# Chunk-selected attention in front of an expert layer: the attention part rewritten from single heads with 128-wide tiles to pairs of heads with 512-wide tiles

## The chip, the cores and the metric

The kernel runs on one core of a Trainium2 chip. The metric is device time in microseconds (us) of one execution. The core has five engines with queues of their own: PE multiplies matrices (its weight loads are listed apart as PEld), DVE and ACT work element by element and can read PE's output memory (PSUM), POOL works element by element on SBUF alone, and SP issues the DMAs. Each works through its queue in order; semaphores make one wait for another.

## The reference, cut to what matters

The first half is attention over 4 batches of 8 heads, 768 positions, head size 64. The keys of a head are cut into 24 chunks of 32. For each query an upper bound of its score with each chunk is made from the chunk's largest and smallest key, and only the six best chunks that are causally allowed are kept.

```python
    k_min = np.min(k_chunks, axis=3)
    k_max = np.max(k_chunks, axis=3)
    ub = np.sum(np.maximum(q[:, :, :, None, :] * k_min[:, :, None, :, :], q[:, :, :, None, :] * k_max[:, :, None, :, :]), axis=-1)
    ub = np.where(causal, ub, -1000000000.0)
    top_chunks = np.argsort(ub, axis=-1)[..., -top_k:]
    mask = sel & (pos[:, None] >= pos[None, :])
    scores = np.where(mask, scores, -1000000000.0)
    ...
    attn = attn / (np.sum(attn, axis=-1, keepdims=True) + 1e-09)
```

The second half takes the 3072 x 512 attention output as `x`: a dense two-layer network, plus one of 8 expert networks per row, chosen by the largest gate logit and weighted by its softmax probability. The kernel computes all 8 experts for all rows and multiplies by a gate vector that is zero except for the chosen one.

## The kernel before, in words

A tile framework orders the instructions of each engine by its own scheduling and puts in the semaphores; the program is fully unrolled. There are three stages, one after the other.

**Attention** (lines 80 to 166) goes head by head, 32 of them. Three DMAs bring q, k and v of a head (L84 to L86), 192 KB each. ACT casts q to float16 (L90), DVE casts k and v (L91, L92); v gets a 65th column of ones (L93), so that the product with it also gives the softmax's sum. PE turns k's six 128-row tiles (L99) and DVE copies each into `lhsT` (L100), whose rows 64 to 87 hold `expand`, which chunk a key belongs to (L96). DVE takes each chunk's maximum and minimum (L103, L108). Then, for each of six query tiles: PE turns q (L117), DVE copies it (L119), ACT makes its positive and negative parts (L121, L122), PE makes the bounds `ub` from them (L126, L127), and DVE selects in eight small instructions of 24 columns (L129 to L138). ACT scales the selection to 0 or -30000 (L140), PE turns it (L143), DVE copies it below the q rows in `rhs` (L144), so that one product gives scores and mask. For each key tile up to the diagonal PE makes 128x128 scores `sp` (L149), ACT takes the exponential `ex` (L154), DVE multiplies the diagonal tile by a triangle (L156), and PE multiplies with v (L157). DVE divides by the sum (L161, L162) into `xbig`.

**Weights** (L168 to L191): 72 pieces of 256 KB and a small one come by DMA into three staging buffers (L183) and are cast to float16 by DVE (L184). The order of every queue has them behind the attention; only the first three DMAs do not wait for a cast.

**Experts** (L193 to the end of the function): for six groups of 512 rows PE turns x (L211), ACT copies it out (L212), and for the dense network and each of 8 experts PE runs 16 products of 512 columns into `hp` (L242), ACT applies relu (L246), PE runs 16 into `yp` (L250), ACT scales by the gate (L258), DVE accumulates (L259). 24 DMAs write the output.

PE's order within a query tile is a chain that leaves PE three times before the first score (to DVE and ACT for `rhs` and `qrel`, to DVE and ACT for `selb`, to DVE for the mask rows of `rhs`); the scheduler interleaves the chains of several tiles, as far as the two or three buffers of each kind allow. A DVE or ACT instruction stands in its queue behind those of the other chains.

Of the kernel before, what the change touches and what calls it, by code (L numbers as in the profile page):

```python
# [8 lines left out]
FP = mybir.dt.float32  # L9
BF = mybir.dt.bfloat16  # L10
HF = mybir.dt.float16
# [6 lines left out]
def kernel(  # L18
# [22 lines left out]
    const = ctx.enter_context(tc.tile_pool(name="const", bufs=1))  # L41

    ident = const.tile([128, 128], HF)
    make_identity(nc, ident)
    identb = const.tile([128, 128], BF)
    make_identity(nc, ident)

    upptri = const.tile([128, 128], HF)
    make_upper_triangular(nc, upptri, 1.0, diag=True)

    expand = const.tile([NC, S], HF)
    nc.gpsimd.memset(expand, 1.0)
    nc.gpsimd.affine_select(out=expand, in_=expand, compare_op=ALU.is_ge, fill=0.0,
                            base=0, pattern=[[1, S]], channel_multiplier=-32)
    nc.gpsimd.affine_select(out=expand, in_=expand, compare_op=ALU.is_ge, fill=0.0,
                            base=31, pattern=[[-1, S]], channel_multiplier=32)

    causal01 = const.tile([128, NT, NC], FP)
    causalbias = const.tile([128, NT, NC], FP)
    nc.gpsimd.memset(causal01, 1.0)  # L60
    nc.gpsimd.affine_select(out=causal01, in_=causal01, compare_op=ALU.is_ge, fill=0.0,
                            base=0, pattern=[[128, NT], [-32, NC]], channel_multiplier=1)
    nc.gpsimd.memset(causalbias, 0.0)
    nc.gpsimd.affine_select(out=causalbias, in_=causalbias, compare_op=ALU.is_ge, fill=NEG,
                            base=0, pattern=[[128, NT], [-32, NC]], channel_multiplier=1)

    xbig = const.tile([128, NM, Dm], HF)

    with (
        tc.tile_pool(name="aload", bufs=3) as aload,  # L70
        tc.tile_pool(name="ahead", bufs=2) as ahead,
        tc.tile_pool(name="aq", bufs=3) as aq,
        tc.tile_pool(name="aexp", bufs=3) as aexp,
        tc.tile_pool(name="pt", bufs=2, space=bass.MemoryType.PSUM) as pt,
        tc.tile_pool(name="psc", bufs=2, space=bass.MemoryType.PSUM) as psc,
        tc.tile_pool(name="pout", bufs=2, space=bass.MemoryType.PSUM) as pout,
        tc.tile_pool(name="psmall", bufs=1, space=bass.MemoryType.PSUM) as psmall,
    ):
        for b in range(B):
            for h in range(H):  # L80
                qf = aload.tile([128, NT, D], FP)
                kf = aload.tile([128, NT, D], FP)
                vf = aload.tile([128, NT, D], FP)
                nc.sync.dma_start(out=qf, in_=q[b, h].rearrange("(t p) d -> p t d", p=128))  # L84
# [30 lines left out]
                for t in range(NT):  # L115
# [31 lines left out]
                    for bb in range(t + 1):  # L147
# [7 lines left out]
                        if bb == t:  # L155
                            nc.vector.tensor_mul(ex, ex, upptri)  # L156
# [140 lines left out]
```

## Time and profile before

| what | value |
|---|---|
| time, median of 2 runs (lowest, highest) | 1068.89 us (1068.28, 1069.51) |
| profiled execution, first to last instruction | 1067.7 us |
| PE busy, matmuls | 790.1 us, 74% |
| DVE busy | 611.5 us, 57% |
| ACT busy | 576.1 us, 54% |
| POOL busy | 4.8 us |
| attention, until the last `xbig` (L162) | 0 to 568 us |
| weights, until PE's first transpose of `xbig` (L211) | 568 to 652 us |
| experts | 652 to 1067.7 us |

The page gives the profiled execution no time beside this span; the median lies 1.2 us above it. Busy time is the union of an engine's instruction spans. The span of an instruction is its own duration, from reading to the write's end; two that follow each other without a wait can overlap, so the spacing of their starts is smaller than the duration. A PE matmul's listed end is modelled. "Clock" is the share of full TensorE speed that was granted, as the profile has it.

### The profile page before, as it was taken

What the parts mean: (1) busy time and instruction counts of PE and PEld (TensorE: products, weight loads), DVE (VectorE), ACT (ScalarE), POOL (GpSimd) and SP (SyncE); (2) the same over time, 40 slices, a digit from 0 to 9 for tenths busy, and PEclk for the clock granted to TensorE, in tenths of its full rate; (3) what the DMA queues carried; (4) which work ended last, traced back from release to release, by engine and by line L of the source; (5) the groups of instructions that cost most, each with busy time, mean ns of one, the idle gap of its engine ahead of it and who ended that gap; (6) DMA issues with size and microseconds to landing.
All of it is one profiled execution on the core that took longest, in us unless ns stands there. A gap on an engine that the chain in (4) does not pass through costs nothing.

```text
span 1067.7 us, 14836 instructions
## 1 busy us (share of the span) xinstructions
PE 790.1 (74%) x4224; PEld 382.4 (36%) x4224; DVE 611.5 (57%) x3297; ACT 576.1 (54%) x1857; POOL 4.8 (0%) x17
## 2 busy tenths in 40 slices
PE   4667767676776767676762005999999999999998
PEld 2333333333333333333330002444444444444443
DVE  6777777877777777777874332433333434433234
ACT  3545544454444445454441003777777777777676
POOL 1000000000000000000000000000000000000000
PEclk9999999999999999999999999999999999999899
DMA  7111111112111111100005772000010010100101
GB/s 178 38 31 45 23 46 28 40 23 45 30 38 31 37 31 38 35 19 1 1 1 150 219 223 86 1 12 28 1 41 1 1 40 1 40 1 1 40 1 40
DMA packets 89699, 45.01 MB, mean 42 GB/s; under 512 B 77329, under 2 KB 77329, under 8 KB 89617
## 3 DMA queue, kind: packets, MB, share of 16 engines
q1 hardware_dynamic: 89616, 44.07, 15.1%
q8 instruction: 33, 0.54, 0.2%
q14 instruction: 50, 0.40, 0.1%
HBM read 37.77 MB, written 6.29 MB: 41 GB/s over the span
## 4 chain that ended last, share of the span: by engine, by line
PE 59%; DVE 19%; ACT 10%; DMA 7%; issue 4%; SPq 0%; ACTq 0%; DVEq 0%
PE hp L242 18%; PE yp L250 17%; PE op L157 7%; DMA s<-in_moe_w_dram 7%; ACT ex L154 6%; PE sp L149 5%; DVE rhs L144 3%; PE qtp L117 3%; PE pst L143 3%; PE tp L99 2%; DVE work L134 2%; ACT selb L140 2%; DVE sel L136 1%; DVE xbig L162 1%; DVE sel L138 1%
## 5 line engine op out<-in xcount | busy, mean ns | idle before, releaser
L259 DVE TENSOR_TENSOR acc<-acc,ts 128x512 f32<-128x512 f32 x192 | 130.8, 693 | 233.5 <-ACT ts L258 233.5
L154 ACT ACTIVATE ex<-sp 128x128 f16<-128x128 f32 x672 | 163.2, 275 | 134.2 <-PE sp L149 118.4
L157 PE MATMUL op<-v_sb,ex 128*128 128x65 f16 x672 | 147.1, 237 | 44.4 <-ACT ex L154 25.4
L149 PE MATMUL sp<-rhs,lhsT 88*128 88x128 f16 x672 | 151.6, 293 | 35.2 <-DVE rhs L144 32.0
L250 PE MATMUL yp<-w2e,hT 128*128 128x512 f16 x768 | 173.6, 379 | 0.0
L242 PE MATMUL hp<-xT,w1e 128*128 128x512 f16 x768 | 173.6, 379 | 0.0
L246 ACT ACTIVATE hT<-hp 128x512 f16<-128x512 f32 x216 | 129.0, 597 | 56.7 <-PE hp L242 56.4
L258 ACT ACTIVATE ts<-yp,gvec 128x512 f32<-128x512 f32 x192 | 130.0, 687 | 40.1 <-PE yp L250 40.1
L250 PEld LDWEIGHTS <-hT 128*128 128x128 f16 x864 | 80.1, 98 | 106.3 <-ACT hT L246 17.1
L157 PEld LDWEIGHTS <-ex 128*128 128x128 f16 x672 | 69.5, 106 | 132.6 <-ACT ex L154 66.3
L140 ACT ACTIVATE selb<-sel 128x24 f16<-128x24 f32 x192 | 42.3, 221 | 125.8 <-DVE sel L138 124.5
L242 PEld LDWEIGHTS <-w1e 128*128 128x128 f16 x768 | 75.2, 98 | 90.6
L143 PE MATMUL pst<-ident,selb 128*24 128x128 f16 x192 | 54.0, 281 | 56.7 <-ACT selb L140 54.3
L211 PE MATMUL tp<-ident,xbig 128*128 128x128 f16 x96 | 19.7, 239 | 94.3 <-ACT xT L212 94.2
L149 PEld LDWEIGHTS <-lhsT 88*128 88x128 f16 x672 | 72.0, 115 | 35.8 <-issue 23.7
L212 ACT ACTIVATE xT<-tp 128x128 f16<-128x128 f16 x96 | 22.3, 275 | 94.1 <-DVE w2e L184 84.9
L99 PE MATMUL tp<-ident,k_sb 128*64 128x128 f16 x192 | 56.9, 306 | 8.2 <-DVE k_sb L91 4.8
L121 ACT ACTIVATE qrel<-qtp 64x128 f16<-64x128 f16 x192 | 50.7, 264 | 20.3 <-DVE rhs L119 20.2
L117 PE MATMUL qtp<-ident,q_sb 128*64 128x128 f16 x192 | 54.9, 301 | 7.4 <-ACT qrel L122 3.6
L144 DVE COPY rhs<-pst 24x128 f16<-24x128 f16 x192 | 41.4, 216 | 25.4 <-PE pst L143 18.7
L156 DVE TENSOR_TENSOR ex<-ex,upptri 128x128 f16<-128x128 f16 x192 | 42.3, 220 | 22.8 <-ACT ex L154 19.6
L162 DVE TENSOR_SCALAR xbig<-op,rs 128x64 f16<-128x64 f32 x192 | 53.6, 279 | 1.0
(62 smaller groups left out, 856.8 us busy)
## 6 DMA issues: line engine op xcount, KB each, us to landing
s<-in_moe_w_dram SPq DMA_DIRECT2D x64, 256.0 KB, 3.1
qf<-in_q_dram SPq DMA_DIRECT2D x32, 192.0 KB, 2.6
kf<-in_k_dram SPq DMA_DIRECT2D x32, 192.0 KB, 2.6
vf<-in_v_dram SPq DMA_DIRECT2D x32, 192.0 KB, 2.6
out_dram<-acc SPq DMA_DIRECT2D x24, 256.0 KB, 2.3
s<-in_moe_w_dense_dram SPq DMA_DIRECT2D x8, 256.0 KB, 2.9
wgs<-in_moe_w_gate_dram SPq DMA_DIRECT2D x1, 16.0 KB, 3.0
```

The lines of the kernel that those rows point to most:

```text
L99: nc.tensor.transpose(tp, k_sb[:, t, :], ident)
L117: nc.tensor.transpose(qtp, q_sb[:, t, :], ident)
L143: nc.tensor.transpose(selTp, selb, ident)
L144: nc.vector.tensor_copy(rhs[D : D + NC, :], selTp)
L149: nc.tensor.matmul(sp, lhsT[:, bb * 128 : (bb + 1) * 128], rhs, start=True, stop=True,)
L154: nc.scalar.activation(ex, sp, AF.Exp, scale=0.125)
L157: nc.tensor.matmul(op, ex, v_sb[:, bb, :], start=(bb == 0), stop=(bb == t))
L242: nc.tensor.matmul(hp, w1ap[:, ko, j * 128 : (j + 1) * 128], xT[:, ko, :], start=(ko == 0), stop=(ko == NK - 1),)
L246: nc.scalar.activation(hT[:, j, :], hp, AF.Relu)
L250: nc.tensor.matmul(yp, hT[:, j, mi * 128 : (mi + 1) * 128], w2ap[:, j, :], start=(j == 0), stop=(j == NK - 1),)
L258: nc.scalar.activation(ts, yp, AF.Copy, scale=gvec[:, mi, e : e + 1])
L259: nc.vector.tensor_add(accs[mi], accs[mi], ts)
```

## The change

The attention part, lines 80 to 166, is written anew for 16 pairs of heads (the diff below shows the core of what is added; what is removed stands in the listing above); weights and experts keep their code and, on every engine, their order.

- **Two heads side by side.** One transpose turns 128 rows of both heads at once (12 per pair for k and q). The chunk statistics of both come from one pair of DVE instructions of 768 columns, read straight from PSUM. Heads are kept apart by zeros: `kb` is masked by `hmask`, and each head has its own `kT` of 128 rows: 64 for k, 24 for the mask (-30000 where a key lies in that chunk), the rest zero.
- **Selection by threshold.** The causal bias comes from a matmul with the identity into the same PSUM tile as the bounds. DVE's MAX takes the eight largest per tile and head (10 per pair), and one comparison per head, "smaller than the sixth", marks the chunks to be masked beside q in `q16`. For each head six transposes (`prep_s`) turn q and mask together, and one DVE copy of 768 columns makes `r`.
- **Packed scores.** The lower triangle's 21 tiles of 128x128 are cut into strips of one key tile and several query tiles, packed into six pieces of 512 columns (the last has 128). ACT takes the exponential of a piece for both heads at once, 1024 columns (256 in the last). POOL zeroes the upper half of the six diagonal tiles (`affine_select`), both heads in one instruction. All 12 outputs of a pair stand in one two-bank PSUM tile `op`, kept in one buffer; one reciprocal and one DVE multiplication of 768 columns normalise them.
- **Pipelined preparation.** While pair p is computed, pair p + 1 is prepared between its steps and pair p + 2 is loaded. POOL does all casts of q, k and v, three instructions of 768 columns per pair.

```diff
...
+    PIECES = [
+        [(0, 0, 512)],
+        [(1, 128, 640)],
+        [(0, 512, 768), (4, 512, 768)],
+        [(2, 256, 768)],
+        [(1, 640, 768), (3, 384, 768)],
+        [(5, 640, 768)],
+    ]
...
+            nc.gpsimd.tensor_copy(k16, s["k"].rearrange("p g t d -> p t g d"))
+            nc.gpsimd.tensor_copy(q16[p % NB][:, :, 64:192].rearrange("p t (g d) -> p t g d", g=2),
+                                  s["q"].rearrange("p g t d -> p t g d"))
+            nc.gpsimd.tensor_copy(v16[p % 3][:, :, :, 0:D], s["v"])
...
+        def prep_k(p):
+            s = st[p]
+            pk = pprep.tile([128, S], HF, name="pp")
+            for t in range(NT):
+                nc.tensor.transpose(pk[:, t * 128 : (t + 1) * 128], s["k16"][:, t].rearrange("p g d -> p (g d)"), ident)
+            ks = ahead.tile([128, 2, NC], HF, name="ks")
+            pkc = pk.rearrange("d (c w) -> d c w", w=32)
+            nc.vector.tensor_reduce(out=ks[:, 0, :], in_=pkc, op=ALU.max, axis=mybir.AxisListType.X)
+            nc.vector.tensor_reduce(out=ks[:, 1, :], in_=pkc, op=ALU.min, axis=mybir.AxisListType.X)
+            s["kb"] = kb = ahead.tile([128, 2, 2, NC], HF, name="kb")
+            nc.vector.tensor_tensor(kb, ks.unsqueeze(2).to_broadcast([128, 2, 2, NC]),
+                                    hmask.unsqueeze(1).to_broadcast([128, 2, 2, NC]), ALU.mult)
+            nc.vector.tensor_copy(kT[p % NB][0][64:128, :], pk[0:64])
+            nc.vector.tensor_copy(kT[p % NB][1][0:64, :], pk[64:128])
...
+            nc.scalar.activation(qp, pq, AF.Relu)
...
+            nc.vector.tensor_single_scalar(qn, pq, 0.0, ALU.min)
...
+            for t in range(1, NT):
+                for g in range(2):
+                    nc.vector.max(out=m8[:, t, g], in_=ub[:, t, g])
...
+                nc.vector.tensor_tensor(q16[p % NB][:, 1:NT, 192 * g : 192 * g + NC], ub[:, 1:NT, g],
+                                        m8[:, 1:NT, g, 5:6].to_broadcast([128, NT - 1, NC]), ALU.is_lt)
...
+                    nc.tensor.transpose(ps[:, t * 128 : (t + 1) * 128], q16[p % NB][:, t, g * 128 : (g + 1) * 128], ident)
...
+                nc.vector.tensor_copy(r, ps)
...
+        def scores(p, i):
+            s = st[p]
+            sp = psc.tile([128, 2, 512], FP, name="sp")
+            wid = sum(z - a for _, a, z in PIECES[i])
+            for g in range(2):
+                o = 0
+                for bb, a, z in PIECES[i]:
+                    nc.tensor.matmul(sp[:, g, o : o + z - a], kT[p % NB][g][:, bb * 128 : (bb + 1) * 128],
+                                     s["r"][g][:, a:z], start=(o == 0), stop=True, skip_group_check=True)
+                    o += z - a
+            ex = aexp.tile([128, 2, 512], HF, name="ex")
+            nc.scalar.activation(ex[:, :, :wid], sp[:, :, :wid], AF.Exp, scale=0.125)
+            o = 0
+            for bb, a, z in PIECES[i]:
+                if a == bb * 128:
+                    nc.gpsimd.affine_select(out=ex[:, :, o : o + 128], in_=ex[:, :, o : o + 128], compare_op=ALU.is_ge,
+                                            fill=0.0, base=0, pattern=[[0, 2], [1, 128]], channel_multiplier=-1)
...
+                    nc.tensor.matmul(op[:, g, t * (D + 1) : (t + 1) * (D + 1)], ex[:, g, c : c + 128],
+                                     v16[p % 3][:, g, bb, :], start=(i == 0 and n == 0),
+                                     stop=(last_of[t] == (i, bb)), skip_group_check=True)
...
+            nc.vector.reciprocal(rs, opv[:, :, :, D : D + 1])
+            nc.vector.tensor_tensor(
+                xbig[:, b * NT : (b + 1) * NT, hp * 128 : (hp + 1) * 128].rearrange("p t (g d) -> p g t d", g=2),
+                opv[:, :, :, 0:D], rs.to_broadcast([128, 2, NT, D]), ALU.mult)
...
+        for p in range(NP):
+            if p + 2 < NP:
+                load(p + 2)
+            nx = p + 1 if p + 1 < NP else None
+            if nx is not None:
+                cast(nx)
+            scores(p, 0)
+            scores(p, 1)
+            if nx is not None:
+                prep_k(nx)
+                prep_q(nx)
+            av(p, 0)
+            scores(p, 2)
+            av(p, 1)
+            if nx is not None:
+                prep_ub(nx)
+            scores(p, 3)
+            av(p, 2)
+            scores(p, 4)
+            av(p, 3)
+            if nx is not None:
+                prep_s(nx)
+            scores(p, 5)
+            av(p, 4)
+            av(p, 5)
+            norm(p)
...
```

The scheduler also reorders this text. In the lists below, line numbers of the kernel before and of the changed one differ; tile names are the program's, with `pp` for the preparation's PSUM tiles.

On DVE, in the middle of the attention before, twelve neighbours belong to five chains:

```order
L144 COPY rhs<-pst_5920 24x128
L134 MATCH_REPLACE work<-m_5965,ub 128x24
L100 COPY lhsT<-tp 64x128
L136 TENSOR_TENSOR sel<-ub,work 128x24
L100 COPY lhsT<-tp 64x128
L156 TENSOR_TENSOR ex<-ex,upptri 128x128
L137 TENSOR_SCALAR sel<-sel 128x24
L103 TENSOR_REDUCE kstats<-lhsT 64x24
L161 RECIPROCAL rs<-op 128x1
L156 TENSOR_TENSOR ex<-ex,upptri 128x128
L162 TENSOR_SCALAR xbig<-op,rs 128x64
L161 RECIPROCAL rs<-op 128x1
```

On DVE in the changed kernel, with the first reduce (L131) ahead of them, these rows are all that it does for a pair in the middle of the attention:

```order
L132 TENSOR_REDUCE ks<-pp 128x24
L136 COPY kT_0_82<-pp 64x768
L134 TENSOR_TENSOR kb<-ks,hmask 128x96
L137 COPY kT_1_83<-pp 64x768
L147 TENSOR_SCALAR qn<-pp 128x768
L162 MAX m_2301<-pp 128x8 x10
L166 TENSOR_TENSOR q_1_85<-pp,m_2301 128x5x24 x2
L177 COPY r_2351<-pp 128x768
L177 COPY r_2360<-pp 128x768
L223 RECIPROCAL rs<-op 128x12
L224 TENSOR_TENSOR xbig<-op,rs 128x2x6x64
```

22 instructions take the place of those of 12 query tiles; the normalisation of a pair stands behind the two copies `r` for the next (in every other pair the reciprocal stands ahead of them).

POOL did nothing after the constants; its queue now, over two pairs in the middle of the attention:

```order
L120 CAST q_0_84<-qf 128x6x128
L119 CAST k_2223<-kf 128x768
L195 AFFINE_SELECT ex<-ex 128x2x128 x6
L120 CAST q_1_85<-qf 128x6x128
L122 CAST v_1_87<-vf 128x12x64
L119 CAST k_2390<-kf 128x768
L195 AFFINE_SELECT ex<-ex 128x2x128 x6
```

Three casts for later pairs have come to stand between the last select of one pair and the first of the next.

On PE, in the middle of the attention before (here with the numbers of the buffers), scores and products with v alternate, each of the latter behind the exponential of an earlier score:

```order
L157 LDWEIGHTS ex_9206
L157 MATMUL op_9203<-v_sb_8974,ex_9206 128x65
L149 LDWEIGHTS lhsT_8979
L149 MATMUL sp_9214<-rhs_9179,lhsT_8979 128x128
L157 LDWEIGHTS ex_9170
L157 MATMUL op_9152<-v_sb_8974,ex_9170 128x65
```

On PE in the changed kernel, at the end of one pair and the beginning of the next, also with numbers:

```order
L175 LDWEIGHTS q16_0_84
L175 MATMUL pp_1184<-ident_58,q16_0_84 128x128
L187 LDWEIGHTS kT0_0_80
L187 MATMUL sp_1225<-r0_1182,kT0_0_80 128x512
L187 LDWEIGHTS kT0_0_80
L187 MATMUL sp_1231<-r0_1182,kT0_0_80 128x512
L128 LDWEIGHTS k16_1221
L128 MATMUL pp_1237<-ident_58,k16_1221 128x128
```

The text puts `prep_s` ahead of the last scores; in the order, 11 of its 12 transposes (L175) have moved behind the pair's last products with v (in every other pair one of these stands behind them), and the next pair's first scores follow them at once.

## Rows read from the trace of the kernel before

**Rows 1.** Four stretches: busy us (and count) of each engine, clock, DMA share, GB/s.

```profile
0.00:20.00 20.00, 7.30 (x41) 3.99 (x41) 12.46 (x75) 7.63 (x26) 4.79 (x17) 1.00 0.87 197
20.00:560.00 540.00, 376.14 (x2232) 196.72 (x2232) 414.13 (x2816) 264.27 (x1237) 0.00 (x0) 1.00 0.13 30
568.00:652.00 84.00, 0.00 (x0) 0.00 (x0) 30.66 (x73) 0.25 (x2) 0.00 (x0) 1.00 0.71 216
659.00:1067.70 408.70, 395.24 (x1882) 176.22 (x1880) 147.68 (x297) 295.08 (x554) 0.00 (x0) 0.97 0.04 16
```

The columns after the stretch's length are PE, PEld, DVE, ACT and POOL.

**Rows 2.** Who waited for whom, 20 to 560 us: total us, times, longest.

```profile
ACT selb L140 <- DVE sel L138: 121.2, 132, 2.4
ACT ex L154 <- PE sp L149: 116.6, 213, 1.5
```

**Rows 3.** Chain that ended last, at the borders of the stages: start, us, what.

```profile
567.68 0.30 DVE xbig L162
...
568.18 0.33 DVE w1d L184
...
651.29 0.44 DVE w2e L184
...
652.08 0.45 PE tp L211 x2
...
657.20 1.71 PE hp L242 x4
...
661.21 3.45 PE yp L250 x16
```

**Rows 4.** Groups by line: output<-input, count, busy us, mean ns, idle before.

```profile
L154 ACT ACTIVATE ex<-sp 128x128 f16<-128x128 f32 x672 | 163.2, 275 | 134.2 <-PE sp L149 118.4 <-PE op L157 4.9
L259 DVE TENSOR_TENSOR acc<-acc,ts 128x512 f32<-128x512 f32 x192 | 130.8, 693 | 233.5 <-ACT ts L258 233.5
L246 ACT ACTIVATE hT<-hp 128x512 f16<-128x512 f32 x216 | 129.0, 597 | 56.7 <-PE hp L242 56.4
L100 DVE COPY lhsT<-tp 64x128 f16<-64x128 f16 x192 | 38.5, 207 | 11.0 <-PE tp L99 10.8
L131 DVE MAX8 m<-ub 128x8 f32<-128x24 f32 x192 | 33.9, 177 | 0.1
L103 DVE TENSOR_REDUCE kstats<-lhsT 64x24 f16<-64x768 f16 x32 | 30.0, 937 | 0.0
L184 DVE CAST w1e<-s 128x512 f16<-128x512 f32 x32 | 13.7, 427 | 22.8 <-DMA s<-in_moe_w_dram 22.8
L91 DVE CAST k_sb<-kf 128x384 f16<-128x384 f32 x32 | 11.1, 348 | 4.5 <-DMA kf<-in_k_dram 4.5
```

**Rows 5.** The same view, POOL's groups.

```profile
L53 POOL TENSOR_SCALAR_AFFINE_SELECT expand<-expand 24x768 f16<-24x768 f16 x1 | 0.8, 817 | 0.0
L52 POOL MEMSET expand<- 24x768 f16 x1 | 0.7, 728 | 0.0
masks.py:199 POOL TENSOR_SCALAR_AFFINE_SELECT ident<-ident 128x128 f16<-128x128 f16 x2 | 0.6, 290 | 0.0
```

**Rows 6.** Instructions in order of time at 9 us: start, us, engine, line.

```profile
9.39 0.94 DVE L103 TENSOR_REDUCE kstats<-lhsT 64x24 f16<-64x768 f16 x1
...
10.26 0.93 DVE L108 TENSOR_REDUCE kstats<-lhsT 64x24 f16<-64x768 f16 x1
```

**Rows 7.** The same view at 75 us, PE and ACT in the attention.

```profile
75.45 0.45 ACT L154 ACTIVATE ex<-sp 128x128 f16<-128x128 f32 x2 [0.27 <-PE sp L149]
...
75.78 0.24 PE L157 MATMUL op<-v_sb,ex 128*128 128x65 f16 x1
...
75.83 0.29 PE L149 MATMUL sp<-rhs,lhsT 88*128 88x128 f16 x1
...
75.92 0.32 PE L157 MATMUL op<-v_sb,ex 128*128 128x65 f16 x2
...
76.04 0.30 PE L149 MATMUL sp<-rhs,lhsT 88*128 88x128 f16 x1
```

More of the change, by code (lines that the diff above doesn't have):

```diff
@@ L41 @@
     const = ctx.enter_context(tc.tile_pool(name="const", bufs=1))
+    HP = H // 2
+    NP = B * HP
     ident = const.tile([128, 128], HF)
     make_identity(nc, ident)
[L45 to L53, printed above, removed]
+    exf = const.tile([128, S], HF)
@@ L54 @@
+    nc.gpsimd.memset(exf[0:32], -30000.0)
+    nc.gpsimd.affine_select(out=exf[0:32], in_=exf[0:32], compare_op=ALU.is_ge, fill=0.0,
                             base=0, pattern=[[1, S]], channel_multiplier=-32)
-    nc.gpsimd.affine_select(out=expand, in_=expand, compare_op=ALU.is_ge, fill=0.0,
+    nc.gpsimd.affine_select(out=exf[0:32], in_=exf[0:32], compare_op=ALU.is_ge, fill=0.0,
                             base=31, pattern=[[-1, S]], channel_multiplier=32)
-    causal01 = const.tile([128, NT, NC], FP)
@@ L59 @@
[L59 to L65, printed above, removed]
-    xbig = const.tile([128, NM, Dm], HF)
+    cbias = const.tile([128, NT, 2, NC], HF)
@@ new lines @@
+    nc.gpsimd.memset(cbias, 0.0)
+    for g in range(2):
+        nc.gpsimd.affine_select(out=cbias[:, :, g, :], in_=cbias[:, :, g, :], compare_op=ALU.is_ge,
+                                fill=-60000.0, base=0, pattern=[[128, NT], [-32, NC]], channel_multiplier=1)
+    hmask = const.tile([128, 2, NC], HF)
+    nc.gpsimd.memset(hmask, 0.0)
+    nc.gpsimd.memset(hmask[0:64, 0, :], 1.0)
+    nc.gpsimd.memset(hmask[64:128, 1, :], 1.0)
+    xbig = const.tile([128, NM, Dm], HF)
+    NB = 2
+    kT = [[const.tile([128, S], HF, name=f"kT{i}_{g}") for g in range(2)] for i in range(NB)]
@@ new lines @@
+    q16 = [const.tile([128, NT, 256], HF, name=f"q16_{i}") for i in range(NB)]
+    v16 = [const.tile([128, 2, NT, D + 1], HF, name=f"v16_{i}") for i in range(3)]
+    for i in range(NB):
+        nc.vector.memset(kT[i][0], 0.0)
+        nc.vector.memset(kT[i][1], 0.0)
+        nc.vector.tensor_copy(kT[i][0][0:32, :], exf[0:32])
+        nc.vector.tensor_copy(kT[i][1][64:96, :], exf[0:32])
+        nc.gpsimd.memset(q16[i], 0.0)
+    for i in range(3):
+        nc.gpsimd.memset(v16[i][:, :, :, D : D + 1], 1.0)
@@ L69 @@
+    PIECES = [
[6 more added lines that the diff above has]
+    ]
+    last_of = {}
+    for pi, pc in enumerate(PIECES):
+        for bb, a, z in pc:
+            for t in range(a // 128, z // 128):
+                last_of[t] = (pi, bb)
     with (
```

156 lines of the change are left out of this document (70 added, 86 removed).

## The prediction

> **What bounds the kernel now.** First the stretches by stage [rows 1]: the experts keep PE busy 395 of 409 us and are not touched. In the attention (20 to 560 us) no engine is full: DVE 414 of 540 us, PE 376, ACT 264. What fills that stage is who waits for whom [rows 2]: ACT's mask scaling for DVE's selection 121 us, the exponentials for the scores 117 us, in waits of at most 2.4 us. So the attention is many short chains across engines in fixed queues, with thousands of small instructions on DVE. Then the chain at the borders [rows 3]: the last `xbig` ends at 568.0, PE's first transpose for the experts starts at 652.1; between them lie 72 weight pieces, DMA and cast in turn. So attention 568.0, weights 84.1, experts 1067.7 - 652.1 = 415.6 us. The orders of the last two are unchanged in the new program, and the first three pieces still come ahead, so I keep 499.7 us for them and work out the attention alone.
>
> **Durations for the new shapes.** ACT takes 275 ns for 128 columns and 597 for 512 [rows 4], so 0.84 per column: 1.03 us for an exponential of 1024, 0.38 for 256, 0.81 for the relu of 768. Two of 128 fit in 0.45 us [rows 7], so the next starts 0.10 before the last one ends. DVE takes 0.94 for a reduce of 768, and the next starts after 0.87 [rows 4, 6]; float32 arithmetic 0.69 for 512, so about 1.04 ns per column above small operations of 0.18: normalising 768 columns takes 0.96, a threshold of 120 columns 0.28. A float16 copy out of PSUM takes 207 ns for 128 columns [rows 4]; above 177 for 24 columns that is nearer to half of 1.04 ns per column than to all of it, so a copy of 768 is 0.21 + 640 x 0.52 = 0.54 us; at the full rate it would be 0.87.
>
> PE: 16 matmuls of 512 columns take 3.45 us, 0.42 ns per column, but four take 1.71 at 657 us, 0.83 per column [rows 3]: the levels of 2.4 and 1.2 GHz. In the attention the clock column reads 1.00 [rows 1], yet 323 columns (65, 128, 65, 65) take 76.04 - 75.78 = 0.26 us [rows 7], 0.80 per column: that is the 1.2 GHz level, whatever the column says.
>
> POOL's casts have no row. Both sides: POOL's select takes 817 ns for 768 columns and 290 for 128, its memset 728 [rows 5], so 0.82 per column if a cast goes like them; not under 0.7, since the memset reads nothing. Above, nothing bounds it; DVE needs 0.43 for 512 and 0.35 for 384 [rows 4], 0.58 for 768, and I let POOL be up to 1.6. I take 0.82, from the nearest row. A select of two diagonal tiles (256 columns) is 0.29 + 128 x 0.82 ns = 0.40.
>
> The Trainium skill ("GPSIMD Engine Reference", Key points) says that for elementwise work DVE is structurally about twice as fast as GpSimd. No run here shows a cast on POOL; by that rule a cast is 2 x 0.58 = 1.17 us, and the sum would be the first rival's.
>
> **Work per pair.** ACT: 5 x 0.93 + 0.28 + 0.71 = 5.6 us. DVE: 2 x 0.87 reduces, 5 x 0.47 copies and the negative part, 10 x 0.11 maxima, 2 x 0.21 thresholds, 0.25 for `kb` and the reciprocal, 0.89 normalising: 6.8 us. PE: scores 21 x 128 x 2 = 5376 columns, 24 transposes 3072, 42 products with v 2730, bounds 288 + 480; 11,946 columns, 5.0 us at 2.4 GHz and 10.0 at 1.2. POOL: 3 x 0.82 + 6 x 0.40 = 4.9. DMA: 6 x 192 KB = 1.18 MB; the first 20 us moved 197 GB/s at a share of 0.87 [rows 1], so 226 at most: 5.2 us. Nothing reaches 10 us but PE at 1.2 GHz; before, a pair took 568 / 16 = 35.5. So no engine's work sets the period; the chain through all of them does.
>
> **The chain of one pair**, PE at 2.4 GHz, from the pair's first score:
> - Three score matmuls of 512 columns and two k transposes (1792 columns): 0.76 us; result and handover 0.2. The first exponential starts at 0.97.
> - ACT in its order: two exponentials and the relu for the next pair, 0.93 + 0.93 + 0.71: the third exponential starts at 3.54, ends at 4.57; the fourth ends at 5.5.
> - PE after the third: products, the fifth scores around nine bound matmuls, five products that wait 0.40 for a select. The fifth exponential starts at 6.25, ends at 7.28; the sixth ends at 7.56, its select at 8.05.
> - PE's queue has `prep_s` behind the last products: six transposes, 0.34 + 0.25 to DVE, the copy `r` 0.54: 9.35, and the next pair's first score starts.
>
> What is hidden: the preparation on DVE (k transposes done at 1.45, reduces, copies, maxima, thresholds) ends at 7.5, 0.6 before PE would take its transposes; normalising (0.96) stands behind `r`, beside the next scores. POOL has three casts between one pair's last select and the next pair's first: q starts when its transposes are done, at -0.3, so the casts end at 3 x 0.82 - 0.3 = 2.2, against the first exponential's end at 2.0: 0.2 late, under the slack of the third scores. For the handovers to and from POOL, which no row shows, I add 0.65 (bounds 0 and 1.3, DVE's being 0.05). Period 10.0 us.
>
> Ahead: POOL's constants took 4.8 us [rows 1]; about 2.2 of them go, small ones of 1.5 and two memsets of 1536 columns (2 x 2 x 0.73 = 2.9) come: 7.0, and with 0.5 for the start k's cast begins at 7.5; the unpipelined preparation (cast 0.8 + 0.9 PE and handover + 1.8 reduces + 1.4 copies + 0.5 + 0.5 bounds + 1.1 maxima + 0.5 + 1.0 + 0.5) gives the first score at 16.5. The last pair has no relu and no transposes behind it: 8.8 with the normalising.
>
> Sum: 16.5 + 15 x 10.0 + 8.8 = 175.3; + 84.1 + 415.6 = 675.0 us of span. The median lies 1.2 over the span, so 676.
>
> **The rivals.**
> - *POOL's casts are dearer.* They then end late for the first select, on which five products and the third scores wait. At 1.17 us: 3.5 - 0.3 = 3.2, 1.2 late, less 0.2 of slack: period 11.0, 691 us; at 1.6: period 12.3, 711. For it: three casts in front of selects in the same queue. Against: POOL's select, which reads, compares and writes, takes 0.82 [rows 5].
> - *PE stays at 1.2 GHz,* as in the attention before: 10.0 us of columns plus about 1 at the pair's border: 11.0, 691 us. For it: the rows at 75 us. Against: when the experts began, PE went from 427 to 216 ns per matmul between 657 and 661 us [rows 3], and at 1.2 GHz the new attention would give it 10 us of columns in 11. The Trainium skill ("TensorE: Matmul & The Clock Gate", What's actually happening) says that the default is throttled and activity releases it; those two rows agree. By it this rival loses.
> - *A tighter pair:* handovers hidden, period 9.0, 661 us. DVE's 6.8 is the floor. Against: PE, ACT and POOL work in turn at the end of a pair.
> - *It doesn't pipeline:* the preparation (7.5) then stands behind the pair instead of beside it, 15.5 a pair, 758 us. Against: the orders show the next pair's reduces between the exponentials.
> - *Slower than before,* by POOL: the three casts are on every pair's chain, and from (568 - 25.3) / 15 = 36.2 us a pair the gain is gone: 3C + 7.5 = 36.2 gives C = 9.6 us for a cast of 768 columns, twelve times the select. At C = 10 the pair is 37.5, the time 1089 us.
>
> **How the numbers follow.** Forecast 0.52; dearer casts 0.20; 1.2 GHz 0.12; tighter 0.12; no pipelining 0.03; slower 0.01. The range 655 to 710 takes in the first four, nearly to their ends; DVE copies at the full rate (0.33 more each, three ahead of the thresholds, one behind: about 0.7 a pair, 687) lie inside. A measurement of this kernel can tell about 2% from no change. Every case but the last is far beyond that: faster 0.985, within 2% 0.005, slower 0.01.
>
> **What would show it.** Right: 15 equal periods near 10 us, attention done near 175, ACT idle longest before the fifth exponential and at a pair's border, a POOL cast of 768 columns near 0.8 us, the weight stage again 84 us. Wrong: a cast over 1.1 us with PE waiting for selects; the spacing of 512-column scores at 0.43 us; DVE over 8 us a pair; a weight stage or expert stage of another length.

## The result, and the profile after

The changed kernel takes 663.69 us (median; 662.93 to 664.45), against 1068.89 before: a ratio of 0.621, 95% interval 0.6185 to 0.6228. The forecast was 676.0 with a range of 655 to 710. So the direction and the size are right, and the forecast is 12.3 us too long.

The same four stretches as in [rows 1], of the kernel after (the columns are those of rows 1):

```profile
0.00:18.00 18.00, 4.00 (x35) 2.90 (x36) 10.96 (x27) 2.09 (x2) 14.08 (x27) 1.00 1.16 197
18.00:164.00 146.00, 111.88 (x1456) 70.82 (x1455) 110.14 (x336) 91.87 (x111) 70.55 (x137) 0.99 0.58 112
164.00:246.50 82.50, 0.00 (x0) 0.00 (x0) 30.46 (x72) 0.27 (x2) 0.00 (x0) 0.50 0.72 219
246.60:662.70 416.10, 401.71 (x1918) 179.29 (x1917) 149.97 (x312) 299.37 (x575) 0.00 (x0) 0.97 0.04 16
```

The last two stretches are those of before (weights 82.8 us from the end of the last normalising at 163.7, experts 416.1): nearly all of the difference lies in the attention, which ended at 568.0 and now ends at 163.7. There PE is now busy 77% of the time (70% before), DVE 75% (77%), ACT 63% (49%) and POOL 48% (nothing): still none is full. Who waits for whom between 20 and 160 us, the answer to [rows 2] (total us, times, longest):

```profile
POOL ex L195 <- ACT ex L191: 57.9, 64, 3.3
ACT ex L191 <- PE sp L187: 56.9, 32, 7.2
```

ACT waited for scores 213 times before, some 14 a pair of heads; now 32 times, about two a pair, and the mask scaling, which waited for the selection, is gone. Where these two waits are, ACT's instructions in order of time show, for the pair whose first score is at 101.03 and the beginning of the next (start, us, instruction, idle before):

```profile
102.04 1.94 ACT L191 ACTIVATE ex<-sp 128x1024 f16<-128x1024 f32 x2 [2.76 <-PE sp L187]
...
104.56 1.96 ACT L191 ACTIVATE ex<-sp 128x1024 f16<-128x1024 f32 x2
106.77 1.30 ACT L191 ACTIVATE ex<-sp 128x1024 f16<-128x1024 f32 x2 [0.25 <-PE sp L187]
110.86 1.02 ACT L191 ACTIVATE ex<-sp 128x1024 f16<-128x1024 f32 x1 [2.79 <-PE sp L187]
...
115.97 1.30 ACT L191 ACTIVATE ex<-sp 128x1024 f16<-128x1024 f32 x2 [0.64 <-PE sp L187]
```

ACT idles 2.8 us at each border between pairs, and before the fifth exponential 0.25 in this pair and 0.64 in the next. The two kinds of pair alternate, 8.82 and 9.17 us long between first exponentials. The chain of waits says what fills the border (start, us, what):

```profile
101.03 0.59 PE sp L187 x2
...
106.77 1.03 ACT ex L191
...
107.86 0.42 POOL ex L195
...
108.32 0.33 PE op L215 x5
...
108.91 0.29 PE pp L175 x5
...
109.23 0.57 DVE r L177
...
109.84 0.59 PE sp L187 x2
```

From the fifth exponential's end at 107.80 the work goes POOL, PE, DVE, PE, ACT in turn: select, last products, the transposes of the next pair's q and mask, the copy `r`, the next scores. The period here is 109.84 - 101.03 = 8.81 us, that of a shorter pair; the mean of all 15 is (155.00 - 18.07) / 15 = 9.13, from PE's rows of the first and of the last pair's scores:

```profile
18.07 1.01 PE L187 MATMUL sp<-r,kT 128*128 128x512 f16 x2
155.00 0.84 PE L187 MATMUL sp<-r,kT 128*128 128x512 f16 x3 [0.28 <-DVE r L177]
```

Two scores of 512 columns take 1.01 us at 18.07 (1.2 GHz) and 0.59 at 101.03 (2.4 GHz): PE reaches the upper level at the start of the attention. It keeps it (0.99 in the stretch) but for one spell, after 4.7 us (60.0 to 64.7) in which PE was busy for 3.2:

```profile
64.72:68.16 3.44, 3.44 (x25) 2.22 (x24) 2.63 (x5) 2.19 (x3) 2.44 (x5) 0.51 0.60 136
```

There the first score, at 64.44, and the first exponential, at 65.97, lie 1.53 us apart, and 1.01 in the pair above. The durations, from the groups by shape between 20 and 160 us:

```profile
L187 PE MATMUL sp<-r,kT 128*128 128x512 f16 x93 | 30.4, 388 | 4.5 <-DVE r L177 4.5
...
L177 DVE COPY r<-pp 128x768 f16<-128x768 f16 x30 | 15.3, 553 | 10.9 <-PE pp L175 10.6
...
L119 POOL CAST k<-kf 128x768 f16<-128x768 f32 x13 | 10.7, 826 | 5.5 <-PE pp L128 5.2
```

### The profile page after: what moved, and what is told of

Read it like the earlier page. It is cut to its first block, busy times and chain, and to the rows that moved or that the text cites. A ratio compares the mean times of both kernels' runs of the same rounds, so it can differ in the third digit from the quotient of the medians.

```text
span 662.7 us, 9164 instructions
## 1 busy us (share of the span) xinstructions
PE 517.6 (78%) x3408; PEld 253.0 (38%) x3408; DVE 301.5 (45%) x745; ACT 393.7 (59%) x689; POOL 84.6 (13%) x164
## 4 chain that ended last, share of the span: by engine, by line
PE 68%; DMA 11%; ACT 10%; DVE 4%; issue 4%; POOL 1%; SPq 0%; ACTq 0%; DVEq 0%; POOLq 0%
PE hp L336 30%; PE yp L344 28%; DMA s<-in_moe_w_dram 11%; ACT ex L191 8%; PE sp L187 3%; PE op L215 3%; PE tp L305 2%; ACT xT L306 1%; DVE r L177 1%; POOL ex L195 1%; PE pp L175 1%; DVE w2e L278 1%; DVE w1e L278 1%; DMA vf<-in_v_dram 1%; ACT ts L352 1%
## 5 line engine op out<-in xcount | busy, mean ns | idle before, releaser
L191 ACT ACTIVATE ex<-sp 128x1024 f16<-128x1024 f32 x96 | 83.1, 923 | 57.2 <-PE sp L187 57.2
L215 PE MATMUL op<-v,ex 128*128 128x65 f16 x672 | 51.4, 196 | 27.9 <-ACT ex L191 23.7
L187 PE MATMUL sp<-r,kT 128*128 128x512 f16 (+3 forms) x256 | 62.0, 313 | 4.5 <-DVE r L177 4.5
L215 PEld LDWEIGHTS <-ex 128*128 128x128 f16 x672 | 31.6, 98 | 56.5 <-ACT ex L191 35.0
L195 POOL TENSOR_SCALAR_AFFINE_SELECT ex<-ex 128x256 f16<-128x256 f16 x96 | 38.2, 406 | 59.2 <-ACT ex L191 59.2
L336 PE MATMUL hp<-xT,w1d 128*128 128x512 f16 x96 | 33.2, 495 | 0.0
L187 PEld LDWEIGHTS <-kT 128*128 128x128 f16 x256 | 20.9, 99 | 6.9 <-issue 6.4
L177 DVE COPY r<-pp 128x768 f16<-128x768 f16 x32 | 16.5, 553 | 11.6 <-PE pp L175 11.2
L344 PE MATMUL yp<-w2d,hT 128*128 128x512 f16 x96 | 21.7, 379 | 0.0
L162 DVE MAX8 m<-pp 128x8 f32<-128x24 f32 x160 | 16.0, 175 | 10.1 <-PE pp L156 10.1
```

Of the source, the lines that this page charges most:

```text
L187: nc.tensor.matmul(sp[:, g, o : o + z - a], kT[p % NB][g][:, bb * 128 : (bb + 1) * 128], s["r"][g][:, a:z], start=(o == 0), stop=True, ski ...
L191: nc.scalar.activation(ex[:, :, :wid], sp[:, :, :wid], AF.Exp, scale=0.125)
L195: nc.gpsimd.affine_select(out=ex[:, :, o : o + 128], in_=ex[:, :, o : o + 128], compare_op=ALU.is_ge, fill=0.0, base=0, pattern=[[0, 2], [ ...
L215: nc.tensor.matmul(op[:, g, t * (D + 1) : (t + 1) * (D + 1)], ex[:, g, c : c + 128], v16[p % 3][:, g, bb, :], start=(i == 0 and n == 0), s ...
L336: nc.tensor.matmul(hp, w1ap[:, ko, j * 128 : (j + 1) * 128], xT[:, ko, :], start=(ko == 0), stop=(ko == NK - 1),)
L344: nc.tensor.matmul(yp, hT[:, j, mi * 128 : (mi + 1) * 128], w2ap[:, j, :], start=(j == 0), stop=(j == NK - 1),)
```

## The experiments

The theory: the gain comes from a short chain of wide instructions per pair, run beside the preparation of the next pair, and what is left of a pair beyond ACT's 5.7 us is handovers at its border. Rivals: an engine's total work sets the period (DVE or POOL), or TensorE's clock makes the gain, or the order in which the program is written. Each kernel below is the changed kernel with one edit, unless it says otherwise; times are medians, and a difference that stands alone is one to 663.7 us.

**The written order undone** (the preparation of a pair directly ahead of its own scores).

```diff
-            if nx is not None:
-                cast(nx)
+            cast(p); prep_k(p); prep_q(p); prep_ub(p); prep_s(p)
             scores(p, 0)
             scores(p, 1)
-            if nx is not None:
-                prep_k(nx)
-                prep_q(nx)
...
```

> Only the written order is undone: each pair's preparation stands directly ahead of its own scores, nothing else changes. Rival (the gain needs the pipelined text): the preparation of 7.5 us stands behind each pair, about 15.5 us per pair, 758 us. Chain theory with buffers deciding: the orders show that nearly every preparation instruction still lands between the previous pair's exponentials, because two buffers are there and the scheduler moves it; the pair stays at 9.1 us and the time between 655 and 675 us.

Measured: 699.21 us, ratio 0.6545 [0.6525, 0.6564]: 35.5 us more, 2.2 per pair. This is neither side's number. The preparation still runs beside the previous pair (a pair takes some 11.5 us, not 15.5), but two things are worse. The rows are the chain at one border, and two pairs in the form of [rows 1] (the clock is the third number from the end):

```profile
82.96 0.95 DVE xbig L224
83.91 0.28 DVE m L162 x3
...
84.47 1.22 PE pp L175 x11
...
85.70 0.59 PE sp L187
```

```profile
97.31:108.12 10.81, 7.22 (x93) 4.47 (x93) 7.27 (x23) 5.77 (x7) 4.81 (x10) 1.00 0.63 159
...
143.24:155.11 11.87, 8.76 (x94) 5.79 (x94) 7.21 (x22) 5.83 (x7) 4.66 (x9) 0.79 0.01 1
```

The scheduler now puts the normalising into DVE's queue among the next pair's maxima, so thresholds, eleven transposes and the scores all wait for it. And PE does not keep 2.4 GHz there: a pair at a granted clock of 1.00 takes 10.8 us, one at 0.79 takes 11.9. So the order alone costs 1.7 us a pair (10.81 against 9.13), and the clock about 1 more where it falls.

**Preparation forced behind the pair.** As the last one, and k's transposes go into the PSUM buffer that the previous pair's outputs hold.

```diff
-            pk = pprep.tile([128, S], HF, name="pp")
+            pk = pout.tile([128, 2048], HF, tag="op", name="pk")[:, :S]
```

> As the run with the written order undone, and the k transposes write into the same single PSUM buffer that the outputs of the previous pair hold until its normalising is done, so the chain of the preparation through k is forced behind the pair. Chain theory: 8.7 us for a pair to its normalising, then transposes 0.35, reduces 1.9, a copy and the masked maxima 0.8, bounds 0.4, maxima 1.1, thresholds 0.5, transposes 0.25, two copies 1.1 = 6.4: 15.1 us per pair, 18.1 + 15 x 15.1 + 8.7 + 82.8 + 416.1 = 752 us (740 to 765). Rival (the work of an engine sets the period, DVE's 6.9 of 9.1 us first of all): the work per engine is unchanged, so the time is too, within 10 us of 664.

Measured: 778.38 us, ratio 0.7288 [0.7274, 0.7302]: 114.7 us more, with the same instructions on each engine. So it is the overlap, not an engine's total, that sets the period; the rival of equal work is refuted by over 100 us. The time is 26 us over what I expected. PE's granted clock is about 0.70 in this attention, and on the chain stand eleven of the transposes L175, not six, so the two groups of transposes cost more than the 0.35 and 0.25 that I took:

```profile
95.06 0.83 PE pk L128 x6
...
100.49 1.35 PE pp L175 x11
```

That is 1.6 us a pair, 24 of the 26 us. So the 115 us contain what the lower clock costs.

**Scores unpacked:** 21 tiles with an exponential each in place of six pieces.

```diff
-        [(0, 0, 512)],
-        [(1, 128, 640)],
...
...
+        flat += [[(bb, t * 128, t * 128 + 128)] for bb, t in tiles]
+    PIECES = flat
...
```

> Scores unpacked: 21 tiles of 128 x 2 x 128 columns per pair, each with its own exponential and its own buffer, in place of six pieces of up to 512 columns. Chain theory: ACT 21 x 0.28 + 0.71 = 6.6 us per pair in place of 5.6, products can begin earlier; the chain through ACT grows by at most that 1.0: 9.1 to 10.1 us per pair, 664 to 680 us. Rival (the gain comes from wide exponentials): 21 handovers of score, exponential and select in turn at about 0.6 us each, 13 us per pair, about 720 us.

Measured: 684.9 us, ratio 0.6414 [0.6402, 0.6427]: 21.2 more, 1.3 per pair. It is 5 us over the chain's range and 35 under the rival's. My price of an exponential of 256 columns was at fault: I took 0.28 us, and ACT is busy 103.2 / 306 = 0.34 with each, 7.1 and not 5.9 us a pair. ACT's group between 30 and 180 us has it:

```profile
L198 ACT ACTIVATE ex<-sp 128x256 f16<-128x256 f32 x306 | 103.2, 385 | 39.2 <-PE sp L194 21.1 <-PE op L222 0.5 <-issue 0.2
```

So the packing is worth 21 us here, a twentieth of the gain.

**POOL's casts issued twice.**

```diff
-            nc.gpsimd.tensor_copy(k16, s["k"].rearrange("p g t d -> p t g d"))
+            for _ in range(2):
+                nc.gpsimd.tensor_copy(k16, s["k"].rearrange("p g t d -> p t g d"))
...
```

The casts of q and v are doubled in the same way.

> Each of POOL's three casts is issued twice; the work repeated changes nothing in the output. Chain theory: POOL has 4.4 us idle per pair of 9.1, but the casts stand in its queue between selects; 2.5 us more of them end the last cast at about 4.7 instead of 2.25 after the first score, the first select and the five products behind it come 1.3 to 2.5 us later: 10.4 to 11.6 us per pair, 683 to 701 us. Rival (POOL is half idle, so it hides it): within 5 us of 664.

Measured: 671.35 us, ratio 0.6283 [0.627, 0.6297]: 7.7 more, 0.5 per pair for 2.5 us of casts. This is nearer to the rival, but outside its 5 us. ACT's and POOL's instructions show why:

```profile
88.75 1.94 ACT L194 ACTIVATE ex<-sp 128x1024 f16<-128x1024 f32 x2 [2.76 <-PE sp L190]
...
89.79 0.83 POOL L125 CAST v<-vf 128x768 f16<-128x768 f32 x1
90.57 0.41 POOL L198 TENSOR_SCALAR_AFFINE_SELECT ex<-ex 128x256 f16<-128x256 f16 x1
90.92 0.83 POOL L120 CAST k<-kf 128x768 f16<-128x768 f32 x1
```

The first exponential (1.03 of the 1.94) ends at 89.78, and the first select starts 0.79 later, behind the doubled casts of q and v; in the changed kernel it starts 0.17 later (103.06 to 103.23). So POOL's casts do delay the select. Most of the 2.5 us is hidden, since the scheduler puts k's two casts between the selects, where POOL has waits.

**The former selection in place of the thresholds** (60 small DVE instructions per pair).

```diff
-                nc.vector.tensor_tensor(q16[p % NB][:, 1:NT, 192 * g : 192 * g + NC], ub[:, 1:NT, g],
-                                        m8[:, 1:NT, g, 5:6].to_broadcast([128, NT - 1, NC]), ALU.is_lt)
+                    nc.vector.memset(m8[:, t, g, 6:8], NEG)
+                    nc.vector.tensor_copy(ubs, ub[:, t, g])
+                    nc.vector.match_replace(out=work, in_to_replace=m8[:, t, g], in_values=ubs, imm_value=NEG)
+                    nc.vector.tensor_sub(sel, ubs, work)
+                    nc.vector.tensor_single_scalar(sel, sel, 1.0, ALU.min)
+                    nc.vector.tensor_scalar(out=..., in0=sel, scalar1=-1.0, scalar2=1.0, op0=ALU.mult, op1=ALU.add)
```

> The two threshold comparisons per pair are replaced by the former selection, per tile and head: fill of two maxima, copy, match and replace, subtract, minimum, multiply-add, 60 small DVE instructions per pair. At the former kernel's durations that is about 5.5 to 6 us of DVE per pair, on the way from the maxima to the transposes of the negated selection. Chain theory with DVE then the bound (6.9 + 5.6 = 12.5 us per pair): 18.5 + 15 x 12.5 + 8.7 + 499 = 714 us at the least; if all of it lies on the chain 14.7 per pair, 747 us. I expect 710 to 750. Rival (selection was never on the path): within 10 us of 664.

Measured: 754.18 us, ratio 0.7061 [0.7039, 0.7082]: 90.5 more. In one pair DVE is busy 12.9 of 14.6 us, 6.0 more than the 6.9 (110.14 / 146 x 9.13) of a pair after:

```profile
82.10:96.70 14.60, 9.74 (x94) 5.47 (x94) 12.91 (x90) 5.77 (x7) 4.87 (x9) 0.73 0.38 83
```

That 6.0 x 15 gives 90 us is partly chance. Between first exponentials a pair takes 14.67 us, 5.6 more than the 9.08 after, and the first one starts 5.8 later (25.57 against 19.76): 15 x 5.6 + 5.8 = 90. Where the 5.6 are, the chain shows, beside DVE's maxima in the changed kernel:

```profile
88.23 1.00 DVE m L162 x10
...
95.22 0.86 DVE xbig L233
...
96.69 1.01 PE sp L196 x2
```

```profile
106.93 1.00 DVE L162 MAX8 m<-pp 128x8 f32<-128x24 f32 x10 [0.67 <-PE pp L156]
```

From the first maximum to the next pair's first score it is 8.46 us here and 109.84 - 106.93 = 2.91 in the changed kernel. DVE fills these 8.46 almost without a break, so the selection is on the chain; but the normalising (0.86) has come to stand among it, and PE's clock fell to 0.73. The 90 us contain these two as well.

**Normalising issued twice.**

```diff
+            for _ in range(2):
                 nc.vector.tensor_tensor(xbig[...], opv[:, :, :, 0:D], rs.to_broadcast([128, 2, NT, D]), ALU.mult)
```

> The normalising multiplication of each pair is issued twice on DVE (0.95 us more per pair); the repeat changes nothing in the output. Chain theory: it stands at the start of the next pair, where DVE next has the k reduces; thresholds end 0.6 us before PE takes them, so 0.3 to 0.4 of it comes through: 5 to 6 us in all, plus 1 at the end, 668 to 672 us. Rival (DVE sets the period): 16 x 0.95 = 15 us, 679 us. Rival (wholly hidden): 664 to 665 us.

Measured: 664.31 us, ratio 0.6223 [0.6209, 0.6237], which overlaps the 0.6185 to 0.6228 of the changed kernel. DVE's work doesn't set the period: 0.95 us a pair would have cost 15. But it isn't hidden wholly, as ACT's instructions show:

```profile
107.12 1.30 ACT L191 ACTIVATE ex<-sp 128x1024 f16<-128x1024 f32 x2 [0.25 <-PE sp L187]
111.53 1.94 ACT L191 ACTIVATE ex<-sp 128x1024 f16<-128x1024 f32 x2 [3.12 <-PE sp L187]
```

The wait at the border is 3.12 in nearly every pair, 0.33 more than the 2.79 above, because the transposes now wait for the thresholds; that is the 0.3 to 0.4 of the chain theory, so the 0.6 of slack in my count holds. In exchange the wait before the fifth exponential is 0.25 in nearly every pair, no longer 0.64 in every other one, and the spell of the lower clock is absent. A steady pair takes 9.14 us against 8.99, the mean of 8.82 and 9.17. That the time hardly moved is thus chance in part.

**A probe of the clock in the kernel before:** one matmul of 512 columns per head.

```diff
+                fill = psc.tile([128, 512], FP, tag="sp", name="fill")
+                nc.tensor.matmul(fill, lhsT[:, 0:128], lhsT[:, 0:512], start=True, stop=True)
+                nc.vector.tensor_copy(fsink, fill[:, 0:1])
```

> The kernel before, plus one matmul of 512 columns per head into a score buffer and a copy of one column of it: a probe of TensorE's clock in its attention. Reading of the rows by columns: 1.2 GHz, so the probe's 512 columns take 0.43 us or more. Rival (the profile's clock column, 1.00, is right): 0.22 us. Time within 1% of 1069 us.

Measured: 1076.84 us (one run, 0.9% over the kernel before, measured beside it), and the probe's group (duration ns min/median/max, first and last start):

```profile
L118 PE MATMUL fill<-lhsT x32: 608/615/615, 9.4 to 558.5; 88*128 88x512 f16 x32
```

615 ns from the first head to the last, against 388 for the same columns in the attention after and 379 in the experts: at all 32 places the kernel before ran at 1.2 GHz, while the profile's clock column reads 1.00 there. Part of the gain is thus the clock, which rose to the upper level at the start of the new attention. How much of the 404 us it is wasn't measured by itself. An estimate from the full chain of the pair at 101.03: PE has 2.8 of its 8.81 us, so the lower level, at twice the time, would add about 2.8 a pair, 42 us or a tenth of the gain. The undone order fits this: a pair lost 1.06 us (11.87 - 10.81) at a clock of 0.79, which is the lower level for 0.42 of the time, so 2.5 for a whole pair.

**Preparation two pairs ahead** (three buffers for it, but two in place of three for the loads; `prep_ub` and `prep_s` of the next pair in the first half of a pair, `prep_k` and `prep_q` of the one after it in the second).

```diff
             scores(p, 1)
+            prep_ub(n1)
             av(p, 0)
...
             scores(p, 3)
+            prep_s(n1)
             av(p, 2)
+            prep_k(n2)
...
+            prep_q(n2)
```

> The preparation runs two pairs ahead instead of one (k and q transposes, reduces and copies two ahead; bounds, thresholds and negated selection one ahead, in the first half of a pair), with three buffers for it. Nothing is left out. Chain theory: the six transposes and the copy that stood behind the last products of a pair (about 1.4 us) and the wait for POOL's last select go off the path; the period falls to what ACT's order or DVE's 6.9 us allow, 7.0 to 8.0: 15 x 1.1 to 2.1 less, 632 to 650 us, with some 3 us more at the start. Rival (the chain through a pair's exponentials and selects alone sets it): within 5 us of 664.

Measured: 660.16 us, ratio 0.6181 [0.6164, 0.6198]: 3.5 less, so near the rival. The transposes did not leave the border. Eleven of them and the copies `r` still stand directly ahead of the pair's first score:

```profile
89.38 0.78 PE L175 MATMUL pp<-ident,q 128*128 128x128 f16 x11
...
89.86 1.02 DVE L177 COPY r<-pp 128x768 f16<-128x768 f16 x2 [1.30 <-PE pp L175]
...
90.90 0.38 PE L187 MATMUL sp<-r,kT 128*128 128x512 f16 x1
```

And a new wait came, the chain has it:

```profile
94.97 0.97 DVE xbig L224
...
95.98 0.41 PE op L215 x8
```

The pair's first products start only at 95.98, 5.1 us after its first score (103.12 - 101.03 = 2.1 in the changed kernel): the scheduler put the previous pair's normalising behind both reduces, three copies and the negative part, and it holds the one output buffer until then.

**The same with the normalising given precedence.**

```diff
-            norm(p)
+            with tc.high_priority():
+                norm(p)
```

> As the run with the preparation two pairs ahead, with one thing more: the reciprocal and the normalising of a pair have precedence in the scheduler, so in DVE's order they stand around the first k reduce and no longer behind both reduces, three copies and the negative part. Nothing is left out. Theory from the chain of that run (products wait for the one output buffer, which the late normalising holds): the wait of some 2 to 3 us at a pair's start goes, the period falls from 8.7 to between 7.2 (DVE's 6.9 with its waits) and 8.0: 15 x 0.7 to 1.5 less, 637 to 650 us. Rival (another chain of the same length stands behind it): within 4 us of 660.

Measured: 667.86 us, ratio 0.6251 [0.6241, 0.626]: 7.7 more than the last, and not less. The theory that this one wait sets the period falls. The chain, from behind the copy `r` to the first exponential:

```profile
102.80 0.49 PE pp L128 x6
...
103.51 0.34 PE pp L143 x6
103.85 0.66 PE sp L187 x3
...
104.59 1.03 ACT ex L191
```

The twelve transposes of the pair after next now stand in PE's queue among the pair's first scores, and ACT is idle for 2.50 us at the border until they are done; the fifth exponential waits 0.70 more, for scores behind bound matmuls and behind products that wait for a select. Moving the preparation only moved its waits.

**The weights beside the attention.** Loaded two or three pieces per pair, in the order of use, with ACT's casts; the last 35 in the first block of the experts.

```diff
+            wcast("act")
+            if p + 1 < NP:
+                wload(min(2 + p % 2, len(pieces)))
...
+            for e in range(E + 1):
+                wload(6)
+                layer(w1s[e], w2s[e], max(e - 1, 0), e == 0)
+                wcast("dve")
```

> The changed kernel with its weights loaded in the order of use, two or three pieces per pair of heads beside the attention (cast by ACT in its idle time), the last 30 or so beside the first block of the experts (cast by DVE). Nothing is left out. Theory (the weight stage of 82.8 us is DMA and cast time that the attention can hide; DMA share there 0.60, ACT idle 3.5 us per pair): 18 + 15 x 9.2 + 8.7 + 416 = 581 us, up to 595 with some lost to ACT's casts before an exponential. Rival (the transfers collide: 1.18 MB + 0.6 MB per pair at the 117 GB/s that the attention moves now): 15 us per pair, 670 us, no gain.

Measured: 574.87 us, ratio 0.5382 [0.5373, 0.5391]: 88.8 less. Two windows:

```profile
20.00:160.00 140.00, 107.00 (x1456) 68.31 (x1455) 113.54 (x342) 110.74 (x152) 68.90 (x136) 1.00 0.88 201
162.00:573.20 411.20, 398.32 (x1906) 177.50 (x1904) 157.16 (x333) 297.26 (x567) 0.00 (x0) 0.97 0.08 29
```

The DMA engines go from a share of 0.58 to 0.88 and from 112 to 201 GB/s, and the attention isn't longer: its last normalising ends at 160.8 in place of 163.7. The 82.8 us of the weight stage are gone, and the transfers cost the attention nothing. The span is 89.5 us shorter; the other 6.7 come from the attention (2.9) and the experts (3.8).

**Both:** weights early, preparation two ahead with the normalising first.

> Both: the preparation two pairs ahead with the normalising first, and the weights beside the attention. Nothing is left out. If the two savings add: the time of the run with early weights less what the run with the normalising first saves, 555 to 575 us. Rival: with a pair of 7.5 us the DMA queues have 1.8 MB to move per pair, 9 us at the 195 GB/s of the first 16 us, so DMA sets the period and the two don't add: within 8 us of the run with early weights alone.

Measured: 577.3 us, ratio 0.541 [0.54, 0.542], 2.4 more than with early weights alone. The number is the rival's, but its reason isn't shown: the deeper preparation with the normalising first gained nothing by itself either, it cost 4.2 us (667.86 against 663.69). The two changes add to within 2 us, and there was no saving to add.

**Weights early, scores ahead of products** (with a fourth buffer for exponentials).

```diff
-            av(p, 0)
             scores(p, 2)
-            av(p, 1)
+            av(p, 0)
...
             scores(p, 3)
-            av(p, 2)
+            av(p, 1)
```

> The kernel with early weights, and within a pair each piece's scores stand ahead of the products of the piece two before it (they stood behind them), with a fourth exponential buffer. Nothing is left out. Theory (what is left of a pair beyond ACT's 5.6 us is waits of the exponentials for scores that stand in PE's queue behind products, which wait for an exponential and POOL's select): the wait of 0.3 us in mid pair goes, the fifth and sixth exponential come about 0.3 earlier and with them the last select, the last products and the border: 8.9 us per pair falls to 8.3 to 8.6, 564 to 571 us. Rival (the border is set by the thresholds and the selection's transposes): within 3 us of 575.

Measured: 570.65 us, ratio 0.5336 [0.5326, 0.5347]: 4.2 less than with early weights alone, the fastest of all. ACT's instructions of one pair:

```profile
97.47 1.94 ACT L221 ACTIVATE ex<-sp 128x1024 f16<-128x1024 f32 x2 [1.99 <-PE sp L217]
99.30 0.82 ACT L175 ACTIVATE qp<-pp 128x768 f16<-128x768 f16 x1
99.99 3.15 ACT L221 ACTIVATE ex<-sp 128x1024 f16<-128x1024 f32 x4
...
105.94 1.02 ACT L221 ACTIVATE ex<-sp 128x1024 f16<-128x1024 f32 x1 [1.77 <-PE sp L217]
```

Six exponentials and the relu now run without a break from 97.47 to 103.14: the wait in mid pair is gone, as the theory says. The order and the fourth buffer weren't tried apart. What remains of the 8.5 us is the border, from the last exponential at 103.14 to the next first one at 105.94.

## Why the prediction was right, and where it was off

- *What bounds the kernel.* Right for the changed kernel: no engine's work sets the period. The run with the preparation forced behind the pair does the same work in 115 us more, and twice the normalising adds 0.15 of its 0.95 us to a steady pair. For the kernel before, this rests on its rows alone.
- *The unchanged stages.* 84.1 and 415.6 forecast, 82.8 and 416.1 measured.
- *The start.* 16.5 forecast, 18.07 measured. k's first cast began at 9.27 us, not 7.5: POOL's constants ahead of it were sized 1.8 too short; the two memsets of 1536 columns were right (1.56 and 1.38, forecast 2.9).
- *The period.* 10.0 forecast, 9.13 measured; this is the term that was mis-sized, 15 x 0.87 = 13.1 us. Most of it is the 0.65 that I added for handovers to and from POOL: a select starts 0.06 after its exponential's end (107.80 to 107.86) and products 0.04 after the select, like DVE's. From the fifth exponential's end to the next first score the forecast had 2.07 without the addition, and the trace has 2.04 (107.80 to 109.84). The forecast's own steps there add up to 0.17 less; the last products, which it names, have no figure. Ahead of that, the third exponential was put at 3.54 after the first score and came at 3.53; the fifth was put at 6.25 and came at 5.74 in one kind of pair and at 6.13 in the other. In the first its scores stand ahead of nine bound matmuls, in the second behind them. So the periods aren't 15 equal ones, and the outcome lies nearest to "a tighter pair" (9.0, 661 us), in which the handovers are hidden; the forecast took the middle of bounds (0 and 1.3) that no row set, and the runs lie at the lower one.
- *The last pair.* 8.8 forecast; 163.7 - 155.0 = 8.7.
- *Sum.* +1.6 - 13.1 - 0.1 - 1.3 + 0.5 = -12.4: 675.0 becomes the 662.7 of the profiled span.
- *POOL's casts.* 0.82 forecast from the select of as many columns, 0.826 measured. By the rule of the Trainium skill ("GPSIMD Engine Reference", Key points) an estimate of 1.17 came out. The measurement decides against it here: POOL's cast of 768 columns takes 1.4 times the 0.58 that is the estimate for DVE from its casts of 384 and 512. The same page's section "Engine selection" says of operations with one input that POOL is roughly at line rate. This fits: 826 / 768 = 1.08 ns per column, where DVE's float32 arithmetic takes 1.04. The rival's price was wrong as well: it charged a dearer cast in full, and the run with twice the casts cost 0.5 us a pair for 2.5 us of casts, as the scheduler moves k's casts behind the first select.
- *DVE's copies out of PSUM.* 0.54 forecast, 0.553 measured.
- *PE at 2.4 GHz.* Right but for the one spell (388 ns for 512 columns), and the reading of the columns against the clock column was right for the kernel before (615 ns).
- *No pipelining, 758 us.* Measured 778 where it was forced. The forecast argued against it from the queues' orders and not from the written text, and rightly so: with the text's order undone the overlap stays. The buffers and the scheduler make it, and the text's order decides over 35 us by where the normalising and the transposes land.

What the runs give for the parts, each taken back by itself: overlap 115 us, threshold selection 90, order 35, packing 21. The first two contain what PE's lower clock cost there. They overlap each other and don't add up to the 404; the rest, wide instructions for two heads, casts and selects on POOL and PE's clock (42 us by the estimate above), wasn't taken apart.

## What to carry to other kernels

Work out the chain of one period from spans and spacing, and don't add a surcharge for handovers that no row shows: put it in the range instead. Adding work to an engine says more than its busy share: with DVE at 75%, 0.95 us more of normalising cost 0.15 in a steady pair, yet 6.0 us more of selection on the chain cost 5.6. And read such a run's waits as well as its time: a wait that grew and one that fell away can hide each other. And when a stage is made denser, look again at the stages that were left alone: the weight loads, 8% of the time before and 12% after, were the next thing to hide and gave 89 us, more than every further rearrangement of the attention.

## What was unexpected in the hardware

- In the attention of the kernel before, the profile's clock column read 1.00 through 540 us, while the probe's matmuls of 512 columns took 615 ns, the 1.2 GHz level; a known shape's duration is the better gauge.
- The granted clock followed the chain: 0.99 in the kernel after, but 0.73 in the pair of the former selection and 0.79 in the late pairs of the undone order, where it made a pair longer again (10.8 to 11.9 us).
- Weight transfers beside q, k and v took the DMA engines to a share of 0.88 and 201 GB/s without a cost to the attention.
